# Two scatters behind GpSimd's last probability remainders, one weight remainder behind expert 0's first block, and other buffers for two gathers

## The chip, the core and the metric

One core of a Trainium2 chip runs the whole program. The metric is the device time of one execution in microseconds, the median of several. TensorE multiplies matrices and accumulates them in PSUM; VectorE (DVE), ScalarE (ACT) and GpSimd (POOL) do elementwise work; SyncE (SP) only issues DMAs here, and GpSimd issues all DMAs with computed row numbers (gathers and scatters). Each engine works through its own instructions in the order in which the program gives them, and waits for the others by semaphores.

## The reference, cut to what matters

Eight batches of eight heads of causal attention (576 positions, head size 64) with a bias from a running sum of `s`; the result, as 4608 rows of 512, goes through a mixture of eight experts in which each row takes the expert with the largest logit.

```python
scores = scale * q @ k.T ; bias = -(cum[:, None] - cum[None, :])
attn = softmax(scores + min(bias, 0), causal)            # per head
x = (attn @ v).transpose(...).reshape(4608, 512)
logits = normalized(x) @ normalized(expert_emb).T / tau
expert_idx = argmax(logits) ; gate_w = softmax(logits)[expert_idx]
for e in range(8):
    out[mask_e] = gate_w[mask_e] * (relu(x[mask_e] @ w1[e]) @ w2[e])
```

## The kernel before, in words

The program has two stages that overlap at their border: attention, head by head, and the experts, one after the other. Products are made from pairs of numbers, a high part and a remainder (`vh` and `vl`, `P` and `PL`, `xH` and `xL`, `wt` twice), and three matmuls stand for one product.

**Attention.** `step(n)` (L1199) runs for heads 3 to 63 (`NH` is 64). It makes the transposed scores of head n (`ta_`, `tb_`), ScalarE's exponentials (L498, L501), and then, with `pv(n - 2)` (L510, matmuls L526 to L528), the product of the probabilities of head n-2 with v, into the one PSUM bank `om`. Before that product may overwrite `om`, DVE must have read the result of the head before out of it: `norm1`, `norm2`, `norm3` (L539, L543, L551). The remainder of the probabilities, `PL = P - high(P)`, is made by `pl_` (L503): on GpSimd at L252 (TENSOR_TENSOR), for part of heads 57 to 61 on DVE at L508. In each step `emm` (L300) makes a piece of v for the pair of heads at hand, ACT copies its high part (L310), and DVE makes its remainder (L311).

**Router.** When a batch of eight heads is done, `router` (L599) picks an expert for each row by small DVE operations (L608 to L656) with one short group of matmuls (`rank0`, L630 to L636), and queues five scatters of 128 or 64 rows into the row list `xs` (L670, on GpSimd's queue). `scatter()` issues one queued scatter; L1315 says how many at the end of each step, and what is left then is issued behind the loop (L1400).

**Weights.** Weight chunks of 128x512 come through SP's queue (`wissue`, L818), are squared on ACT for a norm (`wsq`, L844), are converted on ACT to their high part (`wcv`, L881), and DVE makes the remainder in `wlow` (L886, the instruction is L889). `wlow(k)` takes the k oldest waiting remainders, in order; behind each one the next chunks are given to SP, whose buffers must first be free.

**Border.** The first expert starts with rows that are known early. `xload(e, t)` (L735, instruction L739) gathers 128 rows of tile t of expert e from `xs` into one of three places of `Qx`, place t % 3. `xtr` (L767) transposes them on TensorE, `xch` and `xcl` (L775, L783) copy high part and remainder; `xprep` does all of it, with `xstat` (L748 to L751, L79) for the router's numbers. `xload(0, 2)` waits for the scatters of batch 6 to land in `xs`. Behind the loop the order is: `pv(62)`, the first block of expert 0 (`first_pass(0)`, L915), `pv(63)`, the other seven blocks with the last batch's router among them, `xtr(0, 2)` behind block 5, and then the second pass.

**Experts 0 and 1.** `l2` (L997) makes the second product of one tile (L986) and `l2o` (L990) scales it on DVE into `Kx` (L993) and scatters it to `out` (L994, GpSimd's queue). In expert 0 the preparations of expert 1's tiles stand between: `xprep(1, 2)` in `fifth`, `xprep(1, 0)` and `xprep(1, 1)` in blocks 1 and 5 of its last pass, `xprep(1, 3)` and `xprep(1, 4)` before its last two tiles. Their gathers are issued in the order `xload(1, 2)`, `(1, 0)` in `third`, `(1, 1)` in `fourth`, and `(1, 3)` and `(1, 4)` in those blocks 1 and 5.

Of the kernel before, what the change touches and what calls it, by code (L numbers as in the profile page):

```python
# [31 lines left out]
SCN = [1, 1, 0, 0, 0, 0, 2, 1]  # L32
# [82 lines left out]
def main(ctx, tc, qkh, qkc, vtin, s_in, emb, tau, w1h, w2h, out, shared, nb):  # L115
# [617 lines left out]
            X[("i", e, t)] = (xf[:, i], (IX["gi0"][:, t:t + 1], IX["va0"][:, t:t + 1]) if e + t0 == 0 and t1 < NTL else (IX["gi"][:, e, t:t + 1], IX["va"][:, e, t:t + 1]), L[:, i], ss[:, i], ex[:, :, t - t0])  # L733

    def xload(e, t):  # L735
        x = HT["Qx"][:, XR * (t % 3):XR * (t % 3) + XR]
        early = e == 0 and t < NF
        src = xs[0:SPL if t < 2 else SPM, :] if early else xs
        ins = nc.gpsimd.indirect_dma_start(out=x.bitcast(I32), out_offset=None, in_=src, in_offset=bass.IndirectOffsetOnAxis(ap=X[("i", e, t)][1][0].bitcast(U32), axis=0),  # L739
                                           bounds_check=src.shape[0] - 1, oob_is_err=False).ins  # L740
        X[("r", e, t)] = x
        if early:
            firsts.append(ins)
# [41 lines left out]
    def xprep(e, t, pt=None):  # L785
        xset(e, t)
        x = X[("r", e, t)][:, 0:XW]
        if e > 1:
            if "xr" not in HT:
                HT["xr"] = const.tile([128, 2, 2, 4, 128], F16, tag="KC1", name="xr")  # L790
            rows = x.rearrange("p (q c) -> p q c", q=4)[:, :, 8:136]
            h, l = (HT["xr"][:, t % 2, i] for i in range(2))
            nc.scalar.copy(h, rows)
            nc.vector.tensor_tensor(l, rows, h, op=ALU.subtract)
            for o, r in ((X[("H", e)], h), (X[("L", e)][1], l)):
                nc.sync.dma_start_transpose(o[:, :, 128 * t:128 * t + 128], r.rearrange("p q c -> p (q c)"))
            return xstat(e, t)
        xtr(e, t, pt)
        xcv(e, t)
        xstat(e, t)  # L800
# [85 lines left out]
    def wlow(k=99):  # L886
        for _ in range(min(k, len(lows))):
            q, l, a, s, h = lows.popleft()
            nc.vector.scalar_tensor_tensor(l, a, s, h, op0=ALU.mult, op1=ALU.subtract)  # L889
            wissue(min(q + 15, X.get("hold", 16 * NE)))  # L890
# [308 lines left out]
    def step(n):  # L1199
        m = n + LA - (n < 6)  # L1200
        live = n < NH
        b0, b1, c8 = n // H, n // H + 1, n % H
        prev = n - 1 < NH
        g, c = n // HG, n % HG
        if live and c == 0:
            hset(g + 1)
            if n > 4:
                load(g + 2)
                loadc(g + 2)
        if n == 10:  # L1210
            setup4()
            setup3()
        fslot()
        norm1(n - 3)
        if live:
            ta_(n, m)
        if prev:
            pl_(n - 1, 576, PS(n), "p")
        sr(m, 3)
        norm2(n - 3)  # L1220
        sa(m)
        if live:
            expa(n)
            prep(n, True)
        norm3(n - 3)
        if NH - 7 < n < NH:
            brk[0] = False
            slots(4)
        if live:
            tb_(n)  # L1230
        sr(m, 2)
        if live and n % 2 == 0:
            tbm(n)
        s3(m)
        if live:
            if n % 2:
                tbm(n)
            tbl(n)
        if n < NH - 6 or n >= NH:
            mslot()  # L1240
        if prev and PS(n) < 1600:
            pl_(n - 1, PS(n), 1600, "v")
        if n < NH - 1:
            wlow(1)
        k = n - NH + 8
        if k == 3:
            wsq(8, True)
        if n < NH - 1:
            emm(n)
        sb(n, m)  # L1250
        sbr(m)
        if n < NH:
            tail(n)
        if n == 5:
            s1(10)
            sr(10, 3)
            s2(10)
        if n == 7:
            vscale(1)
        pv(n - 2, [0, 1, 2])  # L1260
        if n == 7:
            fslot()
        if rq:
            rq.popleft()()
        if n == 5:
            sr(10, 2)
            sr(10, 1)
            s3(10)
        pv(n - 2, [3, 4])
        if n == NH - 1:  # L1270
            emm(n)
        if n == 5:
            s4(10)
        if NH - 7 < n < NH:
            mslot()
        if n >= NH - 1:
            for f in (norm1, norm2, norm3):
                f(n - 2)
        if live:
            expb1(n)  # L1280
            if k == 7:
                wsq(13)
            vcp(n, False)
        if k == 3:
            wsum(0)
        aslot()
        if n == 4:
            load(3)
            loadc(3)
        if live:  # L1290
            prep(n, False)
            vcp(n, True)
        if n == NH - 1:
            xcv(0, 0)
            xtr(0, 1, pxs())
            xcv(0, 1)
        if k > 0:
            wsq((0, 2, 5, 8, 9, 10, 11, 14)[k])
            wcv((0, 0, 0, 0, 2, 1, 2, 1, 1, 1, 0)[k], True)
        brk[0] = False  # L1300
        if n < NH - 6:
            slots(4)
        if n in (4, 5, 6):
            vsq(1, ((0,), (1, 2), (3,))[n - 4])
        if H <= n < NH and 2 <= c8 < 6 and b1 < nb:
            vsq(b1, (c8 - 2,))
        if live and c8 == 6 and 1 < b1 < nb:
            vscale(b1)
        if n == 3:
            loadt(1, pair(1))  # L1310
        if H <= n < NH and c8 < 4:
            loadt(b1, c8)
        if n == NH - 9:
            wissue(3)
        for _ in range(SCN[c8] if n < NH - 22 else 2 if NH - 3 < n < NH else 1 + (c8 > 5) + 4 * (n > NH - 6)):  # L1315
            scatter()
        later()
        if live and c == 0:
            addl(g + 1, True)
        if live and c == 1:  # L1320
            addl(g + 1, False)
        mrow1(m)
        if live:
            pl_(n, 0, 576, "p")
# [81 lines left out]
    wlow(1)  # L1406
    first_pass(0)
    wsq(16)
    wlow(1)
    pv(NH - 1, range(5))  # L1410
    wn = wparts()
    wn.pop(0)()
# [77 lines left out]
    def fifth():  # L1490
        size(0)
        xprep(1, 2, pxm())
        wsq(22)
    l2(0, 1, {2: third, 4: partial(l2o, 0, 0, y), 6: fifth})
    l2(0, 2, {2: fourth, 7: l1t})
# [2 lines left out]
    for e in range(NE):  # L1498
        nx = e + 1 < NE
        w2, w1 = 16 * e + 8, 16 * e + 16  # L1500
        for m in range(8):
            l1(m, e, 0 if e else SPM, MAIN)
            if e > 1 and m == 1:
                l2u(e - 1)
            if e == 1 and m == 0:
                l2o(0, NTL - 1, X["y", 0])
            if e and m == 2:
                size(e)
            if e == 1:
                wsq(w2 + (6, 7, 8)[m] if m < 3 else w1 + (0, 0, 0, 1, 4)[m - 3])  # L1510
                if m == 3:
                    wn = wparts()
                    for i, f in enumerate(X[("g", 1, 0)][4]):
                        if i < len(wn):
                            wn[i]()
                        f()
                wcv((1, 2, 1, 2, 2, 2, 2, 0)[m])
            elif e > 1:
                if e == 2 and m == 0:
                    wsq(w2 + 8)  # L1520
                    wnorm()
                if e == 2 and m < 5:
                    wcv(2 if m else 0)
                if e > 2 and m < 4:
                    wcv(2)
                if nx and m > 3:
                    wsq(w1 + 2 * (m - 3))
            if nx and e > 0 and m == 1:
                xinfo(e + 1, 0, NTL)
            if nx and e > 0 and m == 2:  # L1530
                for t in range(3):
                    xload(e + 1, t)
            if e == 0 and m in (2, 4, 6):
                wsq(24 + m // 2)
            if e == 0 and m in (1, 5):
                xprep(1, m // 4, pxm())
                xload(1, 3 + m // 4)
            if e > 1 and m < 4:
                X[("g", e, 0)][m]()
            if e == 1 and m in (0, 4, 7):  # L1540
                X[("g", e, 0)][{0: 0, 4: 2, 7: 3}[m]]()
            if not nx and m == 5:
                nc.gpsimd.drain()
            if not nx and m == 4:
                xf = X[("i", e, NTL - 1)]
                nc.vector.tensor_copy(shared["last"][:, 0:1].bitcast(I32), xf[0])
                nc.vector.tensor_mul(shared["last"][:, 1:2], xf[3], IX["RS"][:, 2 * e + 1:2 * e + 2])
            if nx and e > 0 and m in (5, 7):
                xprep(e + 1, m // 2 - 2)
                xload(e + 1, m // 2 + 1)  # L1550
            if e == 2 and m == 5:
                count()
            if e == 3 and m == 4:
                shared["total"] = nc.values_load(shared["ci"][0:1, NE - 1:NE], min_val=0, max_val=NT // 128)
# [170 lines left out]
```

## Time and profile before

| | us |
|---|---|
| median of 3 runs | 760.83 (760.51 to 762.04) |
| the profiled execution | 760.35 |
| its span, first to last instruction | 758.6 |
| TensorE busy in it | 738.8 (97%) |
| ScalarE, DVE, GpSimd busy | 567.7, 531.3, 396.7 |

A timeline row has the start in us from the span's start, the length in us (of the whole run, where several equal instructions are merged, `x3`), engine, line, operation, output and inputs, and in brackets the idle time of the engine before it with the releaser that the profile names. Where a wait is for several semaphores, the profile names the one that came last by its own records, which need not be the true one. PE is TensorE. Matmuls overlap, so their lengths add up to more than the time they take.

### The profile page before, as it was taken

What the parts mean: (1) busy time and instruction counts of PE and PEld (TensorE: products, weight loads), DVE (VectorE), ACT (ScalarE), POOL (GpSimd) and SP (SyncE); (2) the same over time, 40 slices, a digit from 0 to 9 for tenths busy, and PEclk for the clock granted to TensorE, in tenths of its full rate; (3) what the DMA queues carried; (4) which work ended last, traced back from release to release, by engine and by line L of the source; (5) the groups of instructions that cost most, each with busy time, mean ns of one, the idle gap of its engine ahead of it and who ended that gap; (6) DMA issues with size and microseconds to landing.
All of it is one profiled execution on the core that took longest, in us unless ns stands there. A gap on an engine that the chain in (4) does not pass through costs nothing. (4 is left out here: it accounts for less than half of the span.)

```text
span 758.6 us, 20953 instructions
## 1 busy us (share of the span) xinstructions
PE 738.8 (97%) x7992; PEld 536.2 (71%) x7992; DVE 531.3 (70%) x1818; ACT 567.7 (75%) x1029; POOL 396.7 (52%) x377
## 2 busy tenths in 40 slices
PE   8999999999999999989989999999999999999996
PEld 4799999999999999978555454545454554554554
DVE  8778888888888888898767767565665566745621
ACT  9898989898999999977667878737658578475410
POOL 9997898989897988685323212222221122312011
PEclk9999999999999999999999999999999999999999
DMA  7789879797979797763625956845755657553001
GB/s 151 176 191 193 172 181 204 179 208 170 210 182 207 165 221 164 183 225 138 213 91 182 191 162 195 185 131 151 178 173 132 189 173 194 168 128 96 13 15 58
DMA packets 76002, 124.01 MB, mean 163 GB/s; under 512 B 38823, under 2 KB 39231, under 8 KB 75032
## 3 DMA queue, kind: packets, MB, share of 16 engines
q0 software_dynamic: 19632, 69.69, 39.1%
q1 hardware_dynamic: 56260, 52.84, 25.8%
q8 instruction: 71, 1.16, 0.7%
q14 instruction: 39, 0.32, 0.2%
HBM read 93.99 MB, written 21.49 MB: 152 GB/s over the span
## 5 line engine op out<-in xcount | busy, mean ns | idle before, releaser
L252 POOL TENSOR_TENSOR PL<-P 128x576 f16<-128x576 f32 (+2 forms) x128 | 204.5, 1719 | 13.6 <-ACT P L498 9.1
L915 PE MATMUL pe<-xH,wt 128*128 128x512 f16 (+1 forms) x576 | 153.0, 344 | 0.6 <-PEq L1020 0.5
L994 POOL DMA_INDIRECT out<-Kx,xj x39 | 43.0, 1103 | 201.6 <-DVE Kx L993 164.3
L915 PEld LDWEIGHTS <-wt 128*128 128x128 f16 x960 | 86.0, 98 | 81.6 <-issue 2.0
L526 PE MATMUL om<-vh,P 128*128 128x73 f16 x960 | 106.8, 198 | 2.7 <-DVE xt L551 2.0
L527 PE MATMUL om<-vl,P 128*128 128x72 f16 x960 | 106.2, 196 | 0.0
L528 PE MATMUL om<-vh,PL 128*128 128x73 f16 x960 | 106.0, 197 | 0.0
L739 POOL DMA_INDIRECT Qx<-xs,idx x40 | 47.5, 1188 | 101.8 <-ACT vjunk L844 44.9
L362 PE MATMUL s<-qkb 96*128 96x288 f32 (+4 forms) x272 | 96.2, 368 | 1.9 <-DVE M L370 0.8
L527 PEld LDWEIGHTS <-P 128*128 128x128 bf16 x960 | 94.6, 99 | 3.6 <-issue 3.2
L915 PE MATMUL pe<-xL,wt 128*128 128x512 f16 (+1 forms) x288 | 95.6, 344 | 0.0
L526 PEld LDWEIGHTS <-P 128*128 128x128 bf16 x960 | 93.8, 99 | 0.5 <-DVE xt L551 0.3
L528 PEld LDWEIGHTS <-PL 128*128 128x128 f16 x960 | 93.8, 98 | 0.0
L917 PE MATMUL pxs<-xH,wt 128*128 128x64 f16 x432 | 83.2, 193 | 0.0
L370 DVE CUSTOM_DVE_ANT_0 junk<-s,mS 128x448 bf16<-128x448 f32 (+3 forms) x144 | 73.9, 520 | 5.0 <-PE s L362 2.8
L986 PE MATMUL pxs<-wt,hq 128*128 128x512 f16 x297 | 72.7, 379 | 0.0
L501 ACT ACTIVATE P<-tb 128x1024 f32<-128x1024 f32 x64 | 65.1, 1017 | 3.3 <-PE tb L467 1.9
L986 PEld LDWEIGHTS <-hq 128*128 128x128 f16 x360 | 35.3, 98 | 42.0 <-ACT idx L88 0.3
L917 PEld LDWEIGHTS <-wt 128*128 128x128 f16 x648 | 63.5, 98 | 0.4
L464 PE MATMUL tb<-QC,KC 128*128 128x448 f32 (+3 forms) x256 | 63.3, 306 | 0.0
L460 PE MATMUL tb<-qkb 128*128 128x448 f32 (+3 forms) x256 | 61.2, 287 | 0.0
L889 DVE SCALAR_TENSOR_TENSOR wt<-ring,idx,wt 128x512 f16<-128x512 f32 x80 | 56.8, 745 | 4.8 <-ACT wt L881 4.8
(335 smaller groups left out, 1997.0 us busy)
## 6 DMA issues: line engine op xcount, KB each, us to landing
qkb<-qkh POOLq DMA_DIRECT2D x15, 1216.0 KB, 9.1
ring<-w2h SPq DMA_DIRECT2D x44, 256.0 KB
ring<-w1h SPq DMA_DIRECT2D x36, 256.0 KB
KC<-qkh POOLq DMA_DIRECT2D x14, 576.0 KB, 8.9
QC<-qkh POOLq DMA_DIRECT2D x14, 576.0 KB, 8.5
vT<-vtin SPq DMA_DIRECT2D x24, 320.0 KB
rw<-w1h SPq DMA_DIRECT2D x15, 256.0 KB
rw<-w2h SPq DMA_DIRECT2D x12, 256.0 KB
```

Of the source, the lines that this page charges most:

```text
L252: nc.gpsimd.tensor_tensor(out, a, b_, op=ALU.subtract)
L362: nc.tensor.matmul(out, G[g]["QB"][0:96, h, 128 * i:128 * i + 128], G[g]["KB"][0:96, h, lo:hi], start=True, stop=True)
L370: nc.vector.tensor_tensor_reduce(out=jk, in0=src, in1=ms, scale=1.0, scalar=NEG, op0=ALU.add, op1=ALU.max, accum_out=MP[n // 2][:, n % 2, ...
L460: nc.tensor.matmul(out, G[g]["KB"][:, h, ks:ks + 128], G[g]["QB"][:, h, 64 + qlo:64 + qhi], start=start, stop=False)
L464: nc.tensor.matmul(out, HD[n]["KC"][:, ks:ks + 128], HD[n]["QC"][:, qlo:qhi], start=False, stop=stop)
L501: nc.scalar.activation(HD[n]["P32"][:, 576:1600], HD[n]["tb"], AF.Exp, scale=0.125)
L526: nc.tensor.matmul(out, lh, vh[:, kb], start=(kb == 0), stop=False)
L527: nc.tensor.matmul(out[:, u:u + 72], lh, vl[:, kb], start=False, stop=False)
L528: nc.tensor.matmul(out, ll, vh[:, kb], start=False, stop=(kb == j))
L915: nc.tensor.matmul(h, w[:, 128 * c:128 * c + 128], x[:, c, lo:hi], start=(i == 0), stop=(i == 11))
L917: nc.tensor.matmul(X["a"][:, HALF * m:HALF * m + HALF], w[:, 128 * c:128 * c + 128], x[:, c, hi:hi + HALF], start=(i == 0), stop=(i == 11))
L986: nc.tensor.matmul(y, h, w, start=(m == 0 and k == 0), stop=(m == 7 and k == 2))
```

## The change

Step 63 issues none of the queued scatters (two before); step 62 keeps its two. So GpSimd makes the two remainders of head 63 directly behind those of head 62, and the three scatters of batch 6 that are left follow them. `wlow(1)` is left out of step 62 too (until now only of step 63), and behind expert 0's first block `wlow(2)` stands instead of `wlow(1)`. For expert 1, tile 3 is gathered into place 2 and tile 4 into place 0 of `Qx` (0 and 1 before); `xload(1, 3)` moves up into `fifth`, behind `xprep(1, 2)`, which is ahead of the scatter of expert 0's tile 1, and `xload(1, 4)` takes the place in block 1 that `xload(1, 3)` had.

```diff
     def xload(e, t):
-        x = HT["Qx"][:, XR * (t % 3):XR * (t % 3) + XR]
+        i = t % 3 if e != 1 or t < 3 else (t - 1) % 3
+        x = HT["Qx"][:, XR * i:XR * i + XR]
...
-        if n < NH - 1:
+        if n < NH - 2:
             wlow(1)
...
-        for _ in range(SCN[c8] if n < NH - 22 else 2 if NH - 3 < n < NH else 1 + (c8 > 5) + 4 * (n > NH - 6)):
+        for _ in range(SCN[c8] if n < NH - 22 else 2 if n == NH - 2 else 0 if n == NH - 1 else 1 + (c8 > 5) + 4 * (n > NH - 6)):
             scatter()
...
     first_pass(0)
     wsq(16)
-    wlow(1)
+    wlow(2)
     pv(NH - 1, range(5))
...
         xprep(1, 2, pxm())
+        xload(1, 3)
         wsq(22)
...
             if e == 0 and m in (1, 5):
                 xprep(1, m // 4, pxm())
-                xload(1, 3 + m // 4)
+                if m == 1:
+                    xload(1, 4)
```

## Rows read from the trace of the kernel before

**Rows 1.** The page's first line.
```profile
span 758.6 us, 20953 instructions
```

**Rows 2.** TensorE's waits, whole span: us in total, times, longest.
```profile
PE pxs L767 <- DMA Qx<-xs,idx: 3.0, 1, 3.0
PE om L526 <- DVE xt L551: 2.0, 1, 2.0
```

**Rows 3.** Timeline of TensorE, 337 to 346 us.
```profile
340.31 0.19 PE L526 MATMUL om<-vh,P 128*128 128x73 f16 x1 [1.97 <-DVE xt L551]
...
345.85 0.20 PE L526 MATMUL om<-vh,P 128*128 128x73 f16 x1
```

**Rows 4.** Timeline of DVE, 334 to 339 us.
```profile
334.95 3.87 DVE L889 SCALAR_TENSOR_TENSOR wt<-rw,idx,wt 128x512 f16<-128x512 f32 x1
338.74 0.66 DVE L311 SCALAR_TENSOR_TENSOR vl<-V,sc,vh 128x432 f16<-128x432 f32 x1
```

**Rows 5.** Timeline of GpSimd, 335 to 349 us; two scatters are left out.
```profile
335.24 3.02 POOL L252 TENSOR_TENSOR PL<-P 128x576 f16<-128x576 f32 x2
...
340.97 3.02 POOL L252 TENSOR_TENSOR PL<-P 128x576 f16<-128x576 f32 x2
344.17 0.93 POOL L670 DMA_INDIRECT xs<-xt,pos  x1 [0.17 <-issue]
347.18 1.29 POOL L739 DMA_INDIRECT Qx<-xs,idx  x1 [2.08 <-DMA xs<-xt,pos]
```

**Rows 6.** Instructions of L311, whole span: ns min/median/max, first and last start.
```profile
L311 DVE SCALAR_TENSOR_TENSOR vl<-V,sc,vh x63: 496/646/667, 31.3 to 343.1; 128x432 f16<-128x432 f32 x32, 128x288 f16<-128x288 f32 x31
```

**Rows 7.** Landing: all L739, the L739 of 347.18, all L670 of the span.
```profile
DMA to landing us min/median/max: 3.5/4.2/6.0
...
DMA to landing us min/median/max: 4.7/4.7/4.7
...
DMA to landing us min/median/max: 2.7/3.9/9.3
```

**Rows 8.** Timeline of DVE, 346 to 352 us.
```profile
346.81 0.74 DVE L889 SCALAR_TENSOR_TENSOR wt<-wt,idx 128x512 f16<-128x512 f32 x1
...
351.27 0.19 DVE L623 TENSOR_TENSOR oh<-wsel,idx 128x40 bf16<-128x40 f32 x1
```

**Rows 9.** Timeline of TensorE, 352 to 355 us.
```profile
352.32 0.18 PE L630 MATMUL om<-oh,tri 128*128 128x40 bf16 x1
...
354.20 0.60 PE L767 MATMUL pxs<-ident,Qx 128*128 128x128 f32 x4
```

**Rows 10.** Timeline of TensorE, 385 to 398 us.
```profile
385.45 0.61 PE L767 MATMUL pxm<-ident,Qx 128*128 128x128 f32 x4
...
390.36 1.12 PE L767 MATMUL pxs<-ident,Qx 128*128 128x128 f32 x4 [2.96 <-DMA Qx<-xs,idx]
...
391.34 2.54 PE L986 MATMUL pxs<-wt,hp 128*128 128x512 f16 x6
...
396.31 1.46 PE L986 MATMUL pxs<-wt,hv 128*128 128x512 f16 x6
```

**Rows 11.** Timeline of GpSimd, 374 to 388 us.
```profile
374.79 1.01 POOL L994 DMA_INDIRECT out<-Kx,xj  x1 [0.30 <-issue]
379.66 0.99 POOL L994 DMA_INDIRECT out<-Kx,xj  x1 [3.86 <-DVE xj L79]
380.95 1.04 POOL L739 DMA_INDIRECT Qx<-xs,idx  x1 [0.30 <-issue]
...
386.70 1.04 POOL L739 DMA_INDIRECT Qx<-xs,idx  x1 [0.30 <-ACT xH L775]
```

**Rows 12.** Stretch 390.4 to 393.5: length, busy time per engine, clock, DMA.
```profile
390.40:393.50 3.10, 3.10 (x11) 1.66 (x12) 1.37 (x9) 1.59 (x5) 0.00 (x0) 0.50 0.30 87
```

**Rows 13.** Timelines of DVE and GpSimd near 360.6 us.
```profile
360.75 0.74 DVE L889 SCALAR_TENSOR_TENSOR wt<-ring,idx,wt 128x512 f16<-128x512 f32 x1
...
360.55 0.92 POOL L670 DMA_INDIRECT xs<-xt,pos  x1 [0.30 <-issue]
```

## The prediction, written before the changed kernel ran

> **What bounds the kernel now.** I read the page first: the span is 758.6 us and TensorE is busy for nearly all of it [rows 1], so only TensorE's idle time, and time in which its clock is low, can be won. The second view is the list of TensorE's waits over the whole span, longest first. Two waits stand far above the rest, and each occurred once [rows 2]: 3.0 us before transposes (L767) that wait for the landing of a gather into `Qx`, and 2.0 us before the attention product (L526) that waits for DVE's L551. The diff touches both places, so the rest of the reading is the timelines of the engines around them.
>
> **First stall.** TensorE stands still for 1.97 us before 340.31, that is from 338.34, until DVE's L551 of head 60 has freed `om` [rows 3]. DVE is late because one instruction, the weight remainder L889 that step 62 issues through `wlow(1)`, starts at 334.95 and lasts 3.87 us; head 62's L311 and then head 60's norm start only behind it, at 338.74 [rows 4]. An L889 elsewhere takes 0.74 [rows 8]. GpSimd's view says why: its two remainders of head 62 run from 335.24 to 338.26, and L889 ends about half a microsecond behind them [rows 4, 5]. So L889, with two inputs from SBUF, is held while GpSimd's TENSOR_TENSORs run.
>
> **Second stall.** TensorE idles 2.96 us before 390.36, until the gather of expert 1's tile 3 has landed [rows 10]. GpSimd issued it at 386.70, behind three other indirect DMAs [rows 11]. The output scatters among them are a chain: the one at 379.66 starts 3.86 us after GpSimd fell idle, and the profile names DVE's L79 as its releaser, which works on another tile. I read this wait as one for the landing of the scatter before, at 374.79, since both write `out`; the next scatter waits in the same way. The gather stands in the program behind that third scatter. The stall costs more than its length: from 390.40 to 393.50 the granted clock is 0.50, the 1.2 GHz level [rows 12], after the engine had done nothing since 387.40. Four transposes take 1.12 instead of 0.61, six L986 take 2.54 instead of 1.46 [rows 10]: 0.51 + 1.08 = 1.6 us lost.
>
> **The change, part by part.**
>
> *Weight remainder out of step 62.* The order of L889s stays and each moves one place back. DVE goes on at 334.95 with L311 and the norm. From L311's start to the product is 340.31 - 338.74 = 1.57 us [rows 3, 4]; L311 may start as late as 336.77 and the product still begins at 338.34. Are these held by GpSimd too? L311 and L551 read one of their two inputs from PSUM; over its 63 instances, spread over the whole attention stage in which GpSimd's remainders run, L311 never took over 0.67 [rows 6]. So the stall goes whole: **-1.97**. Next late is nothing on TensorE's path before head 63's product: the head 61 norm, the transposes and ScalarE's copies follow TensorE and move with it.
>
> *Scatters behind the remainders.* Head 63's product starts at 345.85 [rows 3] and would now start at 343.88. Its remainders end at 340.97 + 3.02 = 343.99 in the old order [rows 5], which would be a new wait of some 0.1. Without the two scatters between, they run from 338.26 to 341.28, 2.6 us ahead. Cost on TensorE: 0. The price is on GpSimd's queue: three scatters follow back to back, each near 1 us with 0.3 between, so the last ends near 345.2 where it ended at 345.10 [rows 5]; the gather `xload(0, 2)`, which waits for its landing, goes out near 347.3 instead of 347.18. It landed 4.7 us after its start [rows 7], so 352.0; TensorE needs it at 354.20 - 1.97 = 352.23 [rows 9]. The slack falls from 2.3 to 0.2. Over all 40 gathers landing took 3.5 to 6.0 [rows 7]: wait 0 to 1.1, and I take **+0.1**, near this gather's own row. The Trainium skill ("DMA: Bandwidth & Descriptors", Anatomy of one DMA) fits 2.0 us plus bytes over 436 GB/s for a DMA of this queue; by that an estimate for 128 rows of 2320 bytes is 2.7 us, and the wait would be 0. The row for the same thing has 4.7, so the sum goes by the row.
>
> *The L889 that arrives behind expert 0's first block.* `wlow(2)` puts 0.74 of DVE work ahead of head 63's norm and the last batch's router [rows 8]. TensorE meets that chain at 352.32 (L630), which needs L623, ended at 351.46 [rows 8, 9]. The slack of 0.86 falls to some 0.1, so 0, bounded by 0 and 0.74; with small hand-overs in the blocks behind it I take **+0.1**. The weight loads on SP's queue that wait for these L889s to free their buffers are expert 1's, squared only behind expert 0's second pass: 0. A rule speaks against this place: the Trainium skill ("SBUF — State Buffer", Who interferes with whom) has a DVE instruction with two SBUF inputs contend with a GpSimd instruction that reads SBUF, and the scatters, which read row numbers there, now stand beside these L889s. In this trace an L889 at 360.75 beside the scatter at 360.55 took 0.74, the usual time [rows 13], so I add nothing; by the rule some 0.3 would be lost.
>
> *Buffer places.* Gather (1,3) goes to the buffer of tile (1,2) and is issued right behind that tile's preparation, between the scatters at 374.79 and 379.66, where GpSimd is idle for 3.9 us [rows 11]: start near 376.1, landed by 382.1 even at 6.0, against 387.40 needed. The stall and the low clock go: -2.96 - 1.6 = **-4.56**. Gather (1,4) moves to the place where (1,3) was; at the median landing of 4.2 [rows 7] it is there by 390.9, and it is needed only behind the 24 L986 that start at 391.34, at 387.9 without the stall, and take four times 1.3 at least [rows 10]: 0. What the new gather can hurt is the landing of the scatter at 374.79, on which the next scatter and gather (1,1) at 380.95 wait. At the median landing that gather is there at 385.15, for transposes at 385.45 [rows 7, 10, 11]: slack 0.3. A delay between 0 and 0.6 (over a third of the 1.8 between median and longest gather) costs 0 to 0.3, and I take 0.
>
> **Sum.** -1.97 - 4.56 + 0.1 + 0.1 = -6.3 us. No wait behind the second stall is near the top of TensorE's list, so what follows moves with it and the span goes from 758.6 to 752.3; the profiled execution, 760.35 with what lies around its span, to 754.0. The median of the runs is 760.83, 0.5 above that execution: **754.5**.
>
> **Rivals.**
> 1. *Gather (0,2) takes the first stall's place.* For: its slack is down to 0.2, and one late scatter or weight load moves it. Against: the last scatter ends hardly later, and TensorE's own small delays ahead of it add slack. At the longest landing of a gather, 6.0, and a scatter that is 0.4 late, it lands at 353.7 and TensorE waits 1.5: 754.5 + 1.4 = 755.9.
> 2. *The first stall does not go*, because what holds L889 also holds L311 or the norm. For: GpSimd now works without a break up to 341.28. Against: rows 6. Then 754.5 + 2.0 = 756.5.
> 3. *The second stall stays in part*, at gather (1,1): the scatter at 374.79 lands 0.6 later beside the new gather, and gather (1,1) takes 6.0 instead of 4.2. Price 1.8 + 0.6 - 0.3 = 2.1: 756.6.
> 4. *Slower.* The place of rival 1, but by the scatters: three of them now leave back to back, and the gather waits for the last one to land. Scatters landed after 2.7 to 9.3 us [rows 7]. At 9.3 the last, started near 344.3, lands at 353.6; a gather of 6.0 behind it lands at 359.6, and TensorE stands for 7.4 us, after which the low clock costs 1.6 as at 390.36. Sum 9.0 - 6.4 = +2.6: 763.4. It decides from a landing past some 357. Against: the last scatter before the change was there 2.1 us after its end [rows 5].
>
> **How the numbers follow.** Forecast 754.5 (753.6 to 755.3): 0.70. Rival 1: 0.12. Rival 2: 0.05. Rival 3: 0.07. Rival 4: 0.03. The rest, 0.03, is a result near the old time by something not seen. The range takes in the forecast's bounds and rivals 1 to 3: 753.4 to 756.6. A measurement of this kernel tells about 0.2% from no change, 1.5 us; forecast and rivals 1 to 3 are all beyond it: faster 0.94, same 0.03, slower 0.03.
>
> **What would show it.** In the changed kernel: no L889 above 1 us between 330 and 350; L311 of head 62 near 335; no wait of L526 for L551; GpSimd's four TENSOR_TENSORs as one run of some 6 us; in expert 0's first pass no wait, or one under 1 us, before L767 for `Qx`; near 385 no wait of 3 us and no clock at 0.50 before the end. A wait for `Qx` above 1 us, an L311 over 0.7, or a gap near the old 385 makes the prediction wrong.

## The result, and the profile after

The changed kernel takes 754.03 us (median of 5 runs, 753.46 to 754.85) beside 762.04 for the kernel before (five runs by now; the 760.83 above was the median of the first three). The ratio is 0.9899, 95% interval 0.9883 to 0.9915; here and below a ratio is taken from all runs and need not be the quotient of the two medians. Its profiled execution took 753.46 against 760.35. Lines of the changed file stand one lower from `xload` on: L767 is now L768, L889 is L890, L994 is L995.

The page's first lines, and the longest of TensorE's waits over the whole span (us in total, times, longest):

```profile
span 751.7 us, 20953 instructions
...
PE 736.4 (98%) x7992; PEld 535.5 (71%) x7992; DVE 528.0 (70%) x1818; ACT 567.5 (75%) x1029; POOL 396.2 (53%) x377
```

```profile
PE pm L448 <- DVE es L590: 1.5, 1, 1.5
PE om L207 <- DVE tiny L186: 1.3, 1, 1.3
PE pxs L768 <- DMA Qx<-xs,idx: 0.9, 1, 0.9
```

Both waits of [rows 2] are gone from the top of this list. What is left first belongs to the start of the kernel; the third is new. The span fell by 6.9 us from [rows 1]; 2.4 of it is TensorE's busy time (738.8 on the page of before), most of that the low clock, and the rest is idle time.

The first place, DVE's timeline (start, length, engine, line, operation; idle time and releaser in brackets):

```profile
334.92 0.67 DVE L311 SCALAR_TENSOR_TENSOR vl<-V,sc,vh 128x432 f16<-128x432 f32 x1 [0.19 <-ACT vh L310]
335.77 0.17 DVE L539 TENSOR_SCALAR z<-om 128x5 f32<-128x5 f32 x1 [0.18 <-PE om L528]
...
336.19 0.53 DVE L551 TENSOR_TENSOR xt<-om,z 128x360 f32<-128x360 f32 x1
...
343.23 0.74 DVE L890 SCALAR_TENSOR_TENSOR wt<-rw,idx,wt 128x512 f16<-128x512 f32 x1
...
344.37 0.75 DVE L890 SCALAR_TENSOR_TENSOR wt<-rw,idx,wt 128x512 f16<-128x512 f32 x1
```

Where the 3.87 us L889 stood [rows 4], L311 starts at once, 0.67 long although GpSimd's remainders run beside it, and the norm is through at 336.7, well ahead of the product. GpSimd's timeline in the same place and, behind the dots, in the second one:

```profile
334.94 5.97 POOL L252 TENSOR_TENSOR PL<-P 128x576 f16<-128x576 f32 x4
341.09 1.00 POOL L670 DMA_INDIRECT xs<-xt,pos  x1 [0.17 <-issue]
342.39 0.98 POOL L670 DMA_INDIRECT xs<-xt,pos  x1 [0.30 <-issue]
343.68 1.10 POOL L670 DMA_INDIRECT xs<-xt,pos  x1 [0.30 <-issue]
348.64 1.04 POOL L740 DMA_INDIRECT Qx<-xs,idx  x1 [3.86 <-DMA xs<-xt,pos]
...
374.62 1.03 POOL L740 DMA_INDIRECT Qx<-xs,idx  x1 [0.85 <-ACT vjunk L845]
377.63 1.01 POOL L995 DMA_INDIRECT out<-Kx,xj  x1 [1.97 <-DVE xj L79]
378.94 1.03 POOL L740 DMA_INDIRECT Qx<-xs,idx  x1 [0.30 <-PE pe L963]
```

The four remainders are one run of 5.97 us, three scatters follow, and the gather of tile (0,2) waits 3.86 us for the last of them to land, where it had waited 2.08 [rows 5]. The gather of tile (1,3), the first of the lower three rows, now goes out at 374.62. TensorE's timeline, and then two stretches of the span (length, busy time of TensorE, its weight loads, DVE, ScalarE and GpSimd, granted clock, DMA share, GB/s):

```profile
352.80 0.63 PE L768 MATMUL pxs<-ident,Qx 128*128 128x128 f32 x4 [0.87 <-DMA Qx<-xs,idx]
...
383.06 0.60 PE L768 MATMUL pxm<-ident,Qx 128*128 128x128 f32 x4
384.84 0.60 PE L768 MATMUL pxs<-ident,Qx 128*128 128x128 f32 x4
385.31 1.46 PE L987 MATMUL pxs<-wt,hp 128*128 128x512 f16 x6
```

```profile
383.00:386.00 3.00, 3.00 (x41) 2.62 (x39) 1.86 (x9) 2.98 (x11) 1.63 (x2) 1.00 0.38 120
386.00:389.00 3.00, 3.00 (x16) 1.35 (x15) 2.71 (x18) 2.28 (x7) 0.00 (x0) 1.00 0.24 74
```

The transposes of tile (1,3) start at 384.84 without a wait, the clock stays at 1.00 (2.4 GHz) and six L987 take 1.46 where they took 2.54 [rows 10, 12].

Both kernels run the same 7992 matmuls in the same order, so their starts can be subtracted one by one. The lead of the changed kernel:

| matmul | before | after | lead |
|---|---|---|---|
| L300 of the head before | 333.51 | 333.21 | 0.30 |
| head 61's product (L526) | 340.31 | 337.87 | 2.44 |
| transposes of tile (0,2) | 354.20 | 352.80 | 1.41 |
| L915, end of that block | 358.36 | 356.33 | 2.03 |
| L962 | 380.56 | 378.17 | 2.39 |
| transposes of tile (1,3) | 390.36 | 384.84 | 5.52 |
| sixth L986 behind them | 393.43 | 386.39 | 7.04 |
| last matmul | 752.59 | 745.25 | 7.34 |

The 0.30 ahead of the change is chance, and 0.4 of the last row is lost again behind the last matmul. So the first place gives 2.1, the gather of tile (0,2) takes 1.0 back, of which 0.6 returns within 4 us because small waits behind it close, and the second place gives 3.1 by its wait and 1.5 by its clock.

### The profile page after: what moved, and what is told of

It is laid out like the page before. It is cut to its first block, busy times and chain, and to the rows that moved or that the text cites. A ratio compares the mean times of both kernels' runs of the same rounds, so it can differ in the third digit from the quotient of the medians.

```text
span 751.7 us, 20953 instructions
## 1 busy us (share of the span) xinstructions
PE 736.4 (98%) x7992; PEld 535.5 (71%) x7992; DVE 528.0 (70%) x1818; ACT 567.5 (75%) x1029; POOL 396.2 (53%) x377
## 5 line engine op out<-in xcount | busy, mean ns | idle before, releaser
L995 POOL DMA_INDIRECT out<-Kx,xj x39 | 42.8, 1098 | 196.9 <-DVE Kx L994 161.7
L526 PE MATMUL om<-vh,P 128*128 128x73 f16 x960 | 106.8, 199 | 0.7 <-DVE base L641 0.3
L526 PEld LDWEIGHTS <-P 128*128 128x128 bf16 x960 | 93.7, 99 | 0.5 <-DVE xt L551 0.3
L987 PE MATMUL pxs<-wt,hq 128*128 128x512 f16 x297 | 72.7, 379 | 0.0
L987 PEld LDWEIGHTS <-hq 128*128 128x128 f16 x360 | 35.2, 98 | 41.8
L890 DVE SCALAR_TENSOR_TENSOR wt<-ring,idx,wt 128x512 f16<-128x512 f32 x80 | 56.8, 746 | 4.8 <-ACT wt L882 4.8
```

The source lines that it names most:

```text
L526: nc.tensor.matmul(out, lh, vh[:, kb], start=(kb == 0), stop=False)
L987: nc.tensor.matmul(y, h, w, start=(m == 0 and k == 0), stop=(m == 7 and k == 2))
```

## Experiments

They ran on three chips, four kernels at a time. On one of them the kernel before takes 761.35 us, about as in the result above; on the other two, the slower ones, 767.41 and 766.36. Whether one of them is the chip of the result is not on record. Ratios are always to the kernel before on the same chip, and a chip is named by that kernel's time.

### The weight remainder alone

```
-        if n < NH - 1:
+        if n < NH - 2:
             wlow(1)
...
     wsq(16)
-    wlow(1)
+    wlow(2)
```

> The kernel before with the weight remainder alone moved (out of step 62, wlow(2) behind expert 0's first block); scatters and buffer places as before. My theory: L889 was held by GpSimd's remainders and held DVE's norm in turn, so TensorE's wait for L551 near 340 (1.97 us) goes; head 63's remainders still end near 343.7, so a wait of 0 to 0.3 before head 63's product appears; the third gather of expert 0 goes out as before and is not waited for. Time 1.7 us below before (1.2 to 2.1). Rival: DVE's later instructions are held by GpSimd as well; then the wait stays near 2.0 and the time is that of before.

765.52 beside 767.41, ratio 0.9975 (0.9964 to 0.9986). The 1.9 us are what was expected, but the trace is not. The stall of 1.97 is gone and L311 takes 0.67; a stop of 1.63 us stands instead before head 62's product, so at this place the trace accounts for 0.3 us, not for 1.9. So I ran it again:

> The kernel before with its weight remainder moved and nothing else, once more on this chip. Theory (the first stall of 1.97 us goes whole, the second stays; what stopped TensorE for 1.6 us before head 62's product in the earlier run belongs to the chip): the first stall is gone, no stop stands before head 62's product, the wait of 3 us and the low clock near 390 stay, the time is 1.5 to 2.0 us below the kernel before. Rival (the moved remainder alone makes a new stop of 1.6 us before head 62's product): the stop is there again, and the time is 0 to 0.4 us below.

That was on the other chip of the slower kind: 765.22 beside 766.36, ratio 0.9986 (0.9970 to 1.0001), a gain of 1.1 us between the two forecasts. TensorE's waits, and DVE in front of the stop:

```profile
PE pxs L767 <- DMA Qx<-xs,idx: 1.8, 1, 1.8
PE om L526 <- DVE xt L551: 1.6, 1, 1.6
```

```profile
336.74 0.53 DVE L551 TENSOR_TENSOR xt<-om,z 128x360 f32<-128x360 f32 x1
341.65 0.16 DVE L539 TENSOR_SCALAR z<-om 128x5 f32<-128x5 f32 x1 [4.38 <-PE pxs L767]
```

DVE has been idle for 4.4 us and waits for TensorE, whose last matmul of head 61's product is recorded as over more than 1.5 us before (the ends of matmuls are modelled). So DVE isn't what is late here; the delay arises on TensorE's side, and the trace doesn't say by what. By the stop the rival seemed right so far; the next group speaks against it.

### The scatters' place

The scatters alone, with the weight remainder left in step 62:

```
-        for _ in range(SCN[c8] if n < NH - 22 else 2 if NH - 3 < n < NH else ...):
+        for _ in range(SCN[c8] if n < NH - 22 else 2 if n == NH - 2 else 0 if n == NH - 1 else ...):
             scatter()
```

> The kernel before with the scatters alone moved behind the remainders; L889 stays in step 62. My theory: L889 is held until GpSimd's run of TENSOR_TENSORs ends, now three microseconds later: L889 takes some 6.9 us, TensorE's wait for L551 grows from 2.0 to 5.0, and behind such a stall the granted clock is 0.50 for some 3 us, 1.6 us more: 4 to 5 us above before. If L889 gets in between the remainders of two heads, it ends as before and the time is that of before. Rival: L889 is late by something else, such as its own input; its length stays 3.9 and the time that of before.

771.36 beside 767.41, 4.0 us above by the medians and so at the lower end of what was expected, ratio 1.0041 (1.0025 to 1.0057). DVE's timeline, GpSimd's, and two stretches:

```profile
335.50 6.81 DVE L889 SCALAR_TENSOR_TENSOR wt<-rw,idx,wt 128x512 f16<-128x512 f32 x1
342.23 0.65 DVE L311 SCALAR_TENSOR_TENSOR vl<-V,sc,vh 128x432 f16<-128x432 f32 x1
```

```profile
335.79 5.96 POOL L252 TENSOR_TENSOR PL<-P 128x576 f16<-128x576 f32 x4
```

```profile
338.80:343.70 4.90, 0.09 (x1) 0.00 (x0) 4.83 (x5) 2.09 (x5) 4.42 (x5) 0.98 0.07 13
343.80:347.00 3.20, 3.20 (x47) 3.20 (x47) 0.21 (x2) 0.00 (x0) 1.59 (x2) 0.51 0.88 299
```

L889 lasts as long as GpSimd's run of remainders: 3.87 beside two of them, 6.81 beside four. Its record starts 0.3 us before theirs both times, and it ends half a microsecond behind the last of them: it doesn't get in between two remainders. This is the clearest evidence of the study for what held DVE. It agrees with the Trainium skill ("SBUF — State Buffer", Who interferes with whom), by which a DVE instruction with two SBUF inputs contends with a GpSimd instruction that reads SBUF. TensorE then stands for 4.92 us and runs at 0.51 behind it. So in this kernel the scatters can be moved only together with the weight remainder.

The change without its moved scatters (the same edit undone in the changed kernel):

> The changed kernel with the scatters back where they were (two at the end of step 63). My theory: in the changed kernel the three scatters in a row make the last one land late (4.7 us after its start instead of 2.8) and gather (0,2) with it, which gives the wait of 0.9 us before L768. With the scatters apart this wait goes, and a wait of 0.1 to 0.3 for head 63's remainders comes before its product: 0.3 to 0.8 us faster than the changed kernel at the end of expert 0's first pass. Rival: the move of the scatters is what pays; head 63's product then waits 1 us or more and the kernel is slower than the changed one by as much.

On the chip at 767.41: 762.54, ratio 0.9935 (0.9919 to 0.9952), with a stop of 1.62 before head 62's product again. The changed kernel didn't run on this chip, so the expectation can't be decided there. Beside the changed kernel, on the chip at 761.35:

> The change without its moved scatters once more, now beside the changed kernel on one chip. Theory (the moved scatters save the wait of head 63's product but pay 0.9 us at the gather of tile (0,2), of which 0.6 comes back): no wait at the transposes of tile (0,2), head 63's product waits 0.1 for GpSimd's remainder, the time within 0.5 us of the changed kernel's. Rival (scatters between the remainders cost TensorE 1.6 us before head 62's product, by whatever path): that stop shows again and the time is 1.0 to 1.6 us above the changed kernel's.

> The changed kernel itself once more, as the measure for the runs beside it. Theory (the extra stops of TensorE in the last four runs, among them 1.6 us before head 62's product where only the weight remainder or all but the scatters was changed, belong to the chip they ran on): the ratio to the kernel before is 0.990 again on any chip, and on a chip like the last one TensorE's extra stops of 0.4 to 0.9 us show here too. Rival (the stop of 1.6 us belongs to a scatter that is issued while head 61's product ends, which only the moved scatters avoid): no stop before head 62's product here on any chip, and the ratio is 0.990 or lower.

> The changed kernel with one of the scatters put back at the end of step 63, between the remainders, and two behind them. Theory (the gather of tile (0,2) waits for the last of three scatters that leave back to back, which landed 4.7 us after its start): with two back to back the last lands 3 to 4 us after its start, the wait before the transposes of tile (0,2) falls from 0.9 to 0.3 or less, and the time is 0 to 0.5 us below the changed kernel's. Rival (scatters between the remainders stop TensorE before head 62's product): a stop of 1.6 us there and a time 1 us above the changed kernel's.

| kernel | us | ratio | wait at tile (0,2) |
|---|---|---|---|
| changed kernel | 753.55 | 0.9898 (0.9882 to 0.9915) | 0.71 |
| scatters not moved | 754.50 | 0.9907 (0.9889 to 0.9924) | 0.51 |
| one between, two behind | 754.22 | 0.9908 (0.9889 to 0.9926) | 0.67 |

No wait or stop stands before head 62's or 63's product in any of the three, so the 1.6 us stop is not made by scatters between the remainders as such; it shows on the two slower chips only. The three times can't be told apart: what the moved scatters bring or cost on this chip is below the 1 to 2 us that the intervals leave open, and TensorE's waits show no gain. The last scatter landed 4.0 to 4.2 us after its start in all three, also where only one or two leave back to back. The theory that their own company delays it has fallen.

### What delays the gather of tile (0,2)

The next suspect was the weight loads on SP's queue. The changed kernel issues two of them right behind the start of the last scatter; here they are held back:

```
-    X, WT, HT = {"hold": 22}, {}, {}
+    X, WT, HT = {"hold": 18}, {}, {}
...
             nc.gpsimd.memset(HT["ring"][0:1, 0:1], 0.0)
+            nc.gpsimd.memset(RW[1][0:1, 0:1], 0.0)
```

> The changed kernel with its four weight loads of 343.9 to 346.5 us held back to about 366 us, behind the gathers of expert 1's first tiles (the limit of loads in flight is 18 instead of 22 until then, and a one-word GpSimd write to the first of their buffers stands ahead of them). Theory (the remainders that the change brings together release their buffers at 343.9 and 345.0, and two weight loads of 256 KB run while the last scatter lands, which is what makes its landing 4.0 to 4.7 instead of 2.8 to 3.1): the last scatter lands 2.7 to 3.2 us after its start, the gather of tile (0,2) goes out 1 us earlier, there is no wait before its transposes, and the time is 0.3 to 0.7 us below the changed kernel's. Rival (the scatters' own company, or chance, makes the landing long): landing 4.0 or more, wait 0.5 to 0.9 as before, time unchanged or up to 1 us above, for the loads that now come late.

> The changed kernel once more, as the measure for the runs beside it: ratio to the kernel before 0.990, a wait of 0.7 to 0.9 us before the transposes of tile (0,2), and the last of the three scatters landing 4.0 to 4.7 us after its start.

These ran on the chip at 766.36. The changed kernel took 763.88, ratio 0.9966 (0.9948 to 0.9985), and the one with held loads 765.11, ratio 0.9986 (0.9972 to 1.0000). As a comparison of times this failed: on this chip another stop made the loads late in the changed kernel too. Two stretches of the changed kernel on this chip, then its last scatter, its gather of tile (0,2) and, from SP's timeline, its first weight load:

```profile
344.00:347.50 3.50, 0.73 (x7) 0.50 (x6) 0.91 (x4) 1.45 (x5) 1.43 (x2) 0.92 0.56 184
347.50:350.20 2.70, 2.67 (x45) 2.67 (x45) 2.32 (x4) 0.34 (x3) 2.11 (x4) 0.50 0.37 80
```

```profile
344.80 0.94 POOL L670 DMA_INDIRECT xs<-xt,pos  x1 [0.30 <-issue]
347.79 1.26 POOL L740 DMA_INDIRECT Qx<-xs,idx  x1 [2.05 <-DMA xs<-xt,pos]
```

```profile
348.20 0.33 SPq L833 DMA_DIRECT2D rw<-w1h  x1
```

The same three on the chip at 761.35 (two loads in one row):

```profile
343.47 1.11 POOL L670 DMA_INDIRECT xs<-xt,pos  x1 [0.31 <-issue]
347.77 1.04 POOL L740 DMA_INDIRECT Qx<-xs,idx  x1 [3.19 <-DMA xs<-xt,pos]
```

```profile
343.85 1.48 SPq L833 DMA_DIRECT2D rw<-w1h  x2
```

The expected landing of 4.0 to 4.7 didn't come because the loads didn't. That makes this run the better test of the mechanism: all fourteen traces of the study have this scatter and this gather, and they fall into two groups by when the first weight load follows the scatter's start.

| traces | scatters moved | first load after | second load after | scatter to gather |
|---|---|---|---|---|
| changed kernel, result and 761.35 | yes | 0.4 | 1.5 | 4.96, 4.30 |
| one between, two behind | in part | 0.4 | 1.6 | 4.30 |
| scatters not moved (761.35) | no | 0.5 | 1.6 | 4.47 |
| weight remainder alone, both; scatters not moved (767.41) | no | 1.9 to 2.0 | 3.1 to 3.2 | 3.21 to 3.23 |
| before, and three more with its order here | no | 2.3 to 3.1 | 2.7 to 3.5 | 2.99 to 3.37 |
| scatters alone; changed kernel and held loads (766.36) | yes | none between the two | | 2.98 to 3.01 |

Early loads go with 4.3 to 5.0, late or no loads with 3.0 to 3.4, with or without moved scatters. (Early loads occurred only where the kernel before takes 761 to 762 us.) The loads start early because the weight remainders at 343.23 and 344.37 free their buffers: it is the other half of the change, not the scatters, that makes the gather late.

Are the loads the cause, or those remainders themselves? In the same four traces, and in no other, two L890s stand beside this scatter, 0.4 us before its start and 0.7 behind it. But the scatter at 360.55 in the trace of before, which has an L889 beside it [rows 13] and no load near, landed after 2.7 us. And the scatter near 338.2, the first of step 63, gives a pair on the chip at 761.35: in the kernel before with work for TensorE (below) a load starts 0.45 us behind it, in the one with the scatters not moved there is none. Their landings, in this order:

```profile
DMA to landing us min/median/max: 4.4/4.4/4.4
DMA to landing us min/median/max: 2.9/2.9/2.9
```

(The held L889 reaches 0.4 us into the first.) Busy DMA engines as such don't do it: with the scatters alone the DMA share was 0.91 in the 2 us behind the last scatter's start, and the gather still followed after 3.01. The loads aren't everything either: the scatter at 341.09 in the changed kernel landed after 3.8, and the first load came 2.95 us behind it. So the loads are well supported as the cause, but the run that was to show it, by holding them back, doesn't. The Trainium skill ("DMA: Bandwidth & Descriptors", Latency and other measured facts) has the fixed part of a DMA grow with the load on the memory. The 3.0 to 3.4 against 4.3 to 5.0 here point the same way; whether it is the memory or the DMA engines that the loads and the scatter share, no run tells apart. That holding the loads back gains time where it is needed was not measured.

### The buffer places, and what the second stall is made of

The buffer places alone:

```
-        x = HT["Qx"][:, XR * (t % 3):XR * (t % 3) + XR]
+        i = t % 3 if e != 1 or t < 3 else (t - 1) % 3
+        x = HT["Qx"][:, XR * i:XR * i + XR]
...
         xprep(1, 2, pxm())
+        xload(1, 3)
...
-                xload(1, 3 + m // 4)
+                if m == 1:
+                    xload(1, 4)
```

> The kernel before with the buffer places and the earlier gather (1,3) alone. My theory: the wait of 2.96 us for Qx near 390 and the 3.4 us of granted clock 0.50 behind it both go, nothing else changes; 4.6 us below before (4.2 to 5.0), the wait for L551 stays at 2.0. Rival: the gather put ahead of the output scatters delays gather (1,1); then a wait for Qx of up to 2 us stands in expert 0's last pass and the gain is 2.5 to 4.

763.60 beside 767.41, ratio 0.9954 (0.9938 to 0.9971): 3.8 us by the medians, 0.8 short of what was expected, but the interval reaches to 4.8. No wait for `Qx` is left, which the rival would have had. The second stall isn't equally long in every run that has it (3.2 and 2.2 in the two others on this chip), and how long the kernel before has it here wasn't profiled. TensorE's timeline; the transposes of tile (1,3), the second row, start without a wait:

```profile
388.53 0.60 PE L768 MATMUL pxm<-ident,Qx 128*128 128x128 f32 x4
390.38 0.60 PE L768 MATMUL pxs<-ident,Qx 128*128 128x128 f32 x4
```

Next, the kernel before with work for TensorE inside the second stall:

```
                 if e == 0:
+                    if t == 3:
+                        z = pxm()
+                        for _ in range(12):
+                            nc.tensor.matmul(z, wt(1, 0)[0][:, 0:128], X[("H", 0)][:, 0, 0:MAIN], start=True, stop=True)
                     xprep(1, t, (pxs if t == 3 else pxm)())
```

> The kernel before, with 12 matmuls of 128 columns by 512 ahead of the transposes of tile (1,3), into a PSUM bank that the transposes then overwrite; their result is used nowhere. They keep TensorE at work for 2.5 us of the 2.96 us in which it waits for the gather. Theory (the wait costs 2.96 by itself and 1.6 by the low clock behind it, and the low clock comes from the idle time): the wait stays in that the transposes start as late as before, no stretch behind it is granted 0.50, and the time is 1.6 us below the kernel before. Rival (the low clock belongs to the place, not to the idle time): the clock falls all the same and the time is that of the kernel before, or 0.5 above it.

758.26 beside 761.35, ratio 0.9960 (0.9944 to 0.9977). TensorE's timeline and one stretch:

```profile
387.26 2.75 PE L1565 MATMUL pxm<-xH,wt 128*128 128x512 f16 x12
390.02 0.66 PE L767 MATMUL pxs<-ident,Qx 128*128 128x128 f32 x4
...
390.54 1.46 PE L986 MATMUL pxs<-wt,hp 128*128 128x512 f16 x6
```

```profile
390.00:393.50 3.50, 3.49 (x20) 1.88 (x20) 2.13 (x15) 2.07 (x6) 0.00 (x0) 1.00 0.32 85
```

The transposes start 0.3 earlier than in [rows 10], of which 0.2 was there before them. At the sixth L986 the lead is 1.8 us: 1.5 won by the clock alone. The low clock came from the standing still, not from the place. By the medians the gain is 3.1, above the 2.3 between the two profiled executions; the interval reaches down to 1.75, a little above the 1.6 expected, and what the rest is wasn't followed.

Last, the kernel before without the wait of one output scatter for the landing of the one before:

```
+        if e == 0 and t < 3:
+            for o in outs:
+                tc.declare_no_dep(ins, o, reason=...)
+            outs.append(ins)
```

> The kernel before, in which expert 0's first three output scatters no longer wait for one another's landing (they write different rows, and the wait between them is declared away); gathers and their buffers are as before. Theory (each of these scatters waits for the landing of the one before, and the gather of tile (1,3) stands in GpSimd's queue behind three of them): the scatter of 379.66 goes out at 376 to 378, the gather of tile (1,3) 1.5 to 3.5 us earlier, the wait of 3 us falls to 0 to 1.5 and the low clock behind it goes, the time is 3 to 4.6 us below the kernel before. Rival (the scatter of 379.66 waits for DVE's product, as the profile's releaser says): all these starts within 0.3 us of the old ones, the wait and the time as before.

765.17 beside 766.36, ratio 0.9987 (0.9973 to 1.0000): 1.2 us by the medians, far from the 3 to 4.6 expected. GpSimd's indirect DMAs on this chip, first with the wait (the weight remainder alone), then without:

```profile
380.78 0.98 POOL L994 DMA_INDIRECT out<-Kx,xj  x1 [2.96 <-DVE xj L79]
382.07 1.04 POOL L739 DMA_INDIRECT Qx<-xs,idx  x1 [0.30 <-ACT vjunk L844]
384.61 0.99 POOL L994 DMA_INDIRECT out<-Kx,xj  x1 [1.50 <-DVE hq L948]
387.50 1.04 POOL L739 DMA_INDIRECT Qx<-xs,idx  x1 [1.90 <-DVE hp L922]
```

```profile
380.26 0.98 POOL L994 DMA_INDIRECT out<-Kx,xj  x1 [0.93 <-DVE Kx L993]
383.11 1.04 POOL L739 DMA_INDIRECT Qx<-xs,idx  x1 [1.87 <-ACT vjunk L844]
384.94 0.99 POOL L994 DMA_INDIRECT out<-Kx,xj  x1 [0.79 <-DVE Kx L993]
389.01 1.04 POOL L739 DMA_INDIRECT Qx<-xs,idx  x1 [3.07 <-DVE hp L922]
```

This kernel runs 1.5 us later here (its first stall is still there). The second scatter goes out 2.0 us earlier against that, so the wait for the landing was real. But the gather of tile (1,3), the last row, comes at the same place, now 3.07 us behind the third scatter. By the program it must wait for its buffer, in which tile (1,0) lies; DVE's last read of that tile:

```profile
387.84 0.27 DVE L79 TENSOR_REDUCE xj<-Qx 128x8 f32<-128x64 f32 x1
```

It ends at 388.1, and the gather follows 0.9 later, though the profile names L922 as its releaser. The next gather into a buffer just read, at 388.60 in the trace of before, follows the same kind of read by 0.9 too. In the trace of before the read of tile (1,0) ends at 384.6, so there the gather could have gone out near 385.5 instead of 386.70 [rows 11], and the stall would have lost 1.2 at best. Two things held this gather, one behind the other.

## Why the prediction was right

It forecast 754.5, and 754.0 was measured. That the two lie within 0.5 us is in part luck: the forecast took 6.3 us off a median of 760.83, and the kernel before came out at 762.04 with five runs, so by the medians the change brought 8.0 us. The profiled executions, in which the terms can be read one by one, differ by 6.9.

- *First stall, -1.97.* 2.1 measured. L311 beside four remainders took 0.67, so rival 2 fell; L889 at 6.81 beside four of them shows the cause.
- *Head 63's product, 0.* No wait. The feared 0.1 without moved scatters didn't show either (chip at 761.35), so this edit had no value on the path there.
- *L890 behind expert 0's first block, +0.1.* No wait of TensorE behind DVE there, and L890 took 0.75 beside the scatter of 343.68: scatters don't hold it as remainders do, and the 0.3 that the prediction named beside its sum was not lost.
- *Gather (0,2), +0.1.* **The mis-sized term: 1.0 at the place, 0.4 after 4 us.** The prediction put the gather at 347.3 with a landing of 4.7; it went out at 348.64 and landed 4.0 later. The step that failed is the sentence on the weight loads, which priced them at 0 because nobody soon waits for their data. But they run while the scatter lands: 4.96 us from scatter to gather where it had been 3.01. The order that makes them early, L889s moved and bunched, was in the prediction, and its rival 1 even names a weight load as something that would move this gather; the sum gave that no price. Rival 1 happened in small, by this path.
- *Second stall, -2.96 and -1.6.* 3.1 and 1.5 measured. The work matmuls show that the two parts are separate. That the scatters wait for one another's landing was right, but as the cause it was half: without these waits the buffer would have let the gather go only 1.2 us earlier. The edit removes both, so the sum didn't suffer; a cure for the chain alone would have been overrated, as its expectation was.
- The terms come to -2.1 + 0.4 - 3.1 - 1.5 = -6.3, the forecast's sum; that the errors of 0.1 to 0.3 cancel is luck. The rest of the 6.9 is 0.3 ahead of the change and 0.7 in small waits at L962 and L986, which this study did not follow, less the 0.4 lost at the end.

**Open.** On the chip at 766.36 the change is worth 0.34%, not 1.0%. The second place gains less there, since the wait is 1.8 to 2.0 long in the kernels that have it and no low clock follows. And the first gain turns into a new stop: 2.8 us before head 63's product, longer than the 1.97 that went, in the changed kernel (there with the clock at 0.50 behind it) and in the one with held loads, where DVE's norm waits. By the program it waits for head 62's product, recorded as over at 343.4; the profile names no engine of this core (`remote`):

```profile
346.52 0.16 DVE L539 TENSOR_SCALAR z<-om 128x5 f32<-128x5 f32 x1 [2.93 <-remote]
```

With the weight remainder moved and the scatters between the remainders the stop is 1.6 us and stands before head 62's product, on both slower chips. So it moves with the scatters, and where the kernel before takes 761 to 762 us it isn't there. What in these chips makes TensorE late beside scatters no run tells apart; I leave it open.

## What to carry to other kernels

A DVE instruction with two SBUF inputs should not be started beside a run of GpSimd TENSOR_TENSORs: here it lasted as long as the run (6.81 us beside 5.96, 0.74 without), so look for instances far above their usual length. When an instruction is moved that frees a buffer, ask which load its end sets off and which transfer on the path will be landing then, even if nobody needs the load's data. A late transfer can have two holders one behind the other; before pricing a cure for the first, read when the second lets go.

## What the chip showed beyond that

- A stop of TensorE costs its length and often more. Behind stops of 1.6 to 2.0 us the clock stayed at 1.00 in every trace looked at; behind 2.2 (scatters alone, second place), 2.96, 3.2 and 4.9 us it fell to 0.50, and behind the 2.8 us stop it fell in one kernel and stayed in another. Length isn't all: with the scatters alone it also fell at 367.4, behind stops of 0.9 and 1.1 us with 0.3 us of work between them.
- Chips differ by 0.8% on the same kernel (761.35 to 767.41). On the two slower ones TensorE makes stops of 0.4 to 1.4 us in the expert stage, most of them put down to "issue" by the profile, some of them beside GpSimd's indirect DMAs: from the start of each of the 39 output scatters to 0.6 us behind its end, TensorE's idle time sums to 1.9 to 2.9 us in each of their eight traces, at three or four scatters in each, and to 0.6 or less in the other six. That the DMAs cause these stops was not tested.
